# A spectral mixer and token MLP: Fourier transform along the sequence first, two global barriers, and an inverse that is streamed block by block into the first MLP tiles

## The chip, the cores and the metric

One core of one Trainium2 chip. The metric is the device time of one execution in microseconds (us), taken as the median of several executions on the same chip. The profile's span is about 2 us shorter than that time. A median below is over all four runs of a kernel. The record marks some of them as slow (over 1.5% above the fastest of the same kernel). A "look" is a single run, whose state is unknown. The experiments ran on three chips, on which the kernel before took 169.06 to 169.16 us.

Names used: PE is the matrix engine (TensorE), DVE the vector engine, ACT the scalar engine, POOL GpSimd, SP the engine used here to issue DMAs. SBUF is the on-chip working memory, PSUM the one that matmuls write to, and an eviction is the pass that brings a result from PSUM to SBUF. In chains, a name with q (ACTq) is the engine's instruction queue, here issuing a DMA and not computing, and "issue" is time for which the profile shows no wait. A barrier is a point at which a stage needs every block of the stage before.

## The reference

The input `x` has S = 2048 rows (sequence) and D = 512 columns. In short:

```python
h  = x + irfft2(rfft2(layernorm(x)) * (w_r + 1j * w_i))      # 2-D transform over S and D
n  = layernorm(layernorm(h))                                 # over D
u  = gelu(einsum("sd,sf->df", n, w1) + b1)                   # F = 1376, contracts over S
h2 = h + transpose(u @ w2 + b2)                              # back to S
```

In the kernels a row is s = 16·p + s2: partition p (128 of them) holds 16 rows, and most work goes by "s2 block" of 128 x 512 elements.

## The kernel before

It transforms along D first (matrix `E`, after transposing X on TensorE), then along S in two steps (`FP`, `G2`) with a second set of transposes between them, multiplies by the weights in SBUF, and goes back by `Hm`, `IFP` and `GD`. The residual is added by an extra matmul with the identity. A small list scheduler in the file fixes each engine's instruction order at build time. So at run time each engine works its list in order: in e6_early (below) DVE stood 7.56 us before a small conversion, and once that was moved back in the list (e8_bias_last) the addition behind it started at 60.4 us instead of 64.1. The parts that matter here:

```python
# statistics of X on DVE, 16 of them; apply is folded into the eviction of the first transform
K.op(f"ln{which}_stats{s2}", "dve", ... eng.bn_stats(st[:, s2, 0:6], src) ...)
...
# spectral multiply: six SBUF-to-SBUF passes for each quarter
K.op(f"wm{q}_t1", "dve", ... eng.tensor_tensor(o, a, b, ALU.mult) ...)   # Cr * Wr
... # t2, t3, t4
K.op(f"wm{q}_r", "dve", ... eng.tensor_tensor(o, a, b, ALU.subtract) ...)
K.op(f"wm{q}_i", "dve", ... eng.tensor_tensor(o, a, b, ALU.add) ...)
...
# weights: natural layout, 128 partitions, pieces of 257 elements (514 bytes)
dma("ld_wr", Wn[:, 0, :, :], A_w_r.rearrange("(k2 k1) k -> k1 k2 k", k1=NP), 1 << 20, stream="sp", ...)
dma("ld_wi", Wn[:, 1, :, :], A_w_i.rearrange("(k2 k1) k -> k1 k2 k", k1=NP), 1 << 20, stream="sp", ...)
...
# second norm: statistics for all 16 blocks, then apply on DVE or ACT, then MLP 1 tile by tile
K.op(f"ln23_apply{s2}", ("dve", "act"), emit_app, ...)
for t in range(NFT):            # 11 tiles of F
    for s2 in range(NS2):       # 16 matmuls of 512 columns, one PSUM bank
        K.op(f"mm1_{t}_mm{s2}", "pe", ...)
    ... # GELU on ACT and DVE
for s2 in range(NS2): ...       # MLP 2: 11 matmuls, one DVE pass, one store
```

Of the kernel before, what the change touches and what calls it, by code (L numbers as in the profile page):

```python
# [8 lines left out]

S_LEN = 2048
D_LEN = 512
NP = 128
NS2 = 16
NKC = 32
F_LEN = 1376
NFT = 11
GELU_C = 0.7978845608028654
LN_EPS = 1e-5


def _bf16(a):
    return np.asarray(a, dtype=np.float32).astype(dt.np(dt.bfloat16))


def build_consts():
    c = {}
    two_pi = 2.0 * np.pi
    d = np.arange(D_LEN)[:, None]
    k = (np.arange(256)[None, :] + 1)  # L30
    ang = two_pi * ((k * d) % D_LEN) / D_LEN
    E = np.concatenate([np.cos(ang), -np.sin(ang)], axis=1)
    c["E"] = E.reshape(4, NP, 512).transpose(1, 0, 2)
    n1 = np.arange(NP)[:, None, None]
    n2 = np.arange(NS2)[None, :, None]
    k1 = np.arange(NP)[None, None, :]
    s = 16 * n1 + n2
    ang = two_pi * ((k1 * s) % S_LEN) / S_LEN
    FP = np.zeros((NP, NS2, 3, NP), np.float64)
    FP[:, :, 0, :] = np.cos(ang)  # L40
    FP[:, :, 1, :] = -np.sin(ang)
    FP[:, :, 2, :] = np.sin(ang)
    c["FP"] = FP
    c["ID"] = np.eye(NP)
    G = np.zeros((NP, 3, NP), np.float64)
    for n2_ in range(NS2):
        for k2_ in range(NS2):
            a = two_pi * ((n2_ * k2_) % NS2) / NS2
            for kk in range(8):
                G[n2_ * 8 + kk, 0, k2_ * 8 + kk] = np.cos(a)  # L50
                G[n2_ * 8 + kk, 1, k2_ * 8 + kk] = -np.sin(a)
                G[n2_ * 8 + kk, 2, k2_ * 8 + kk] = np.sin(a)
    c["G2"] = G
    Hm = np.zeros((NP, 2, 256), np.float64)
    for k2_ in range(NS2):
        for s2_ in range(NS2):
            a = two_pi * ((k2_ * s2_) % NS2) / NS2
            hre, him = np.cos(a), np.sin(a)
            for kk in range(8):
                p = k2_ * 8 + kk  # L60
                col = s2_ * 8 + kk
                Hm[p, 0, col] = hre
                Hm[p, 0, 128 + col] = him
                Hm[p, 1, col] = -him
                Hm[p, 1, 128 + col] = hre
    c["Hm"] = Hm
    k1 = np.arange(NP)[:, None, None]
    s2 = np.arange(NS2)[None, :, None]
    s1 = np.arange(NP)[None, None, :]
    ang = two_pi * ((k1 * (16 * s1 + s2)) % S_LEN) / S_LEN  # L70
    ifr = np.cos(ang) / S_LEN
    ifi = np.sin(ang) / S_LEN
    IFP = np.zeros((NP, NS2, 2, 256), np.float64)
    IFP[:, :, 0, 0:128] = ifr
    IFP[:, :, 0, 128:256] = ifi
    IFP[:, :, 1, 0:128] = -ifi
    IFP[:, :, 1, 128:256] = ifr
    c["IFP"] = IFP
    kk = (np.arange(256)[:, None] + 1)
    dd = np.arange(D_LEN)[None, :]  # L80
    ang = two_pi * ((kk * dd) % D_LEN) / D_LEN
    fac = np.full((256, 1), 2.0 / D_LEN)
    fac[255, 0] = 1.0 / D_LEN
    Gc = fac * np.cos(ang)
    Gs = -fac * np.sin(ang)
    Gs[255, :] = 0.0
    GD = np.zeros((NP, 2, 2, D_LEN), np.float64)
    for half in range(2):
        GD[:, half, 0, :] = Gc[half * 128:(half + 1) * 128, :]
        GD[:, half, 1, :] = Gs[half * 128:(half + 1) * 128, :]  # L90
    c["GD"] = GD
    return c


_ENG_TYPE = {
    "pe": mybir.EngineType.PE,
    "act": mybir.EngineType.Activation,
    "dve": mybir.EngineType.DVE,
    "pool": mybir.EngineType.Pool,
    "sp": mybir.EngineType.SP,  # L100
}
_STREAMS = ["sp", "pe", "act", "dve", "pool"]
N_DMA_SEMS = 36
SB_CELL = 32
# [4 lines left out]
PSUM_BANKS = 8  # L109
PSUM_BANK_BYTES = 2048  # L110


class PsumUnit:

    def __init__(self, name, nbanks=1, early_ok=False):
        self.name = name
        self.nbanks = nbanks
        self.early_ok = early_ok
        self.bank = None
        self.ops = []  # L120
        self.claimed = False
        self.done = False


class Op:
    __slots__ = ("idx", "name", "engines", "stream", "lane", "reads", "writes", "dur", "emit",
                 "psum_unit", "psum_banks", "psum_is_first", "psum_is_last", "deps", "consumers",
                 "sched", "start", "finish", "eng", "increments", "lane_idx", "waits", "prio",
                 "bytes", "is_dma", "_psum_read", "_psum_write", "same_engine_as", "not_before")

    def __init__(self):
        self.deps = []
        self.consumers = []
        self.sched = False
        self.increments = False
        self.lane_idx = None
        self.waits = []
        self.psum_unit = None
        self.psum_banks = []
        self.psum_is_first = False  # L140
        self.psum_is_last = False
        self.prio = 0
        self.bytes = 0
        self.is_dma = False
        self._psum_read = False
        self._psum_write = False
        self.same_engine_as = None
        self.not_before = 0.0


class KernelBuilder:
    def __init__(self, nc):
        self.nc = nc
        self.ops = []
        self.cells = {}
        self.psum_cells = {}
        self.tensors = {}
        self.tensors_by_hname = {}
        self.inst_names = {}
        self.arena_base = None  # L160

    def setup_memory(self, layout, es):
        nc = self.nc
        base = ((nc.sbuf_base + 511) // 512) * 512
        total = nc.sbuf_top - base
        total = (total // 512) * 512
        self.arena_base = base
        self.arena_size = total
        self._slab = es.enter_context(nc.sbuf_tensor("arena_slab", [NP, total - 64], dt.uint8))
        for name, shape, dty, off in layout:  # L170
            size = int(np.prod(shape[1:])) * dt.size(dty)
            assert off % 32 == 0, (name, off)
            assert off + size <= total - 64, f"{name} overflows arena: {off}+{size} > {total}"
            h = nc.alloc_sbuf_tensor_at(name, list(shape), dty, offset=base + off)
            self.tensors[name] = (h, off, off + size)
            self.tensors_by_hname[h.name] = (h, off, off + size)
        return {n: self.tensors[n][0] for n in self.tensors}

    def sb_cells(self, ap):
        t = ap.tensor  # L180
        name = t.name
        if name not in self.tensors_by_hname:
            raise KeyError(name)
        h, lo, hi = self.tensors_by_hname[name]
        esz = dt.size(ap.dtype)
        offs = np.array([int(ap.offset)], dtype=np.int64)
        dims = list(ap.ap)[1:]
        for step, n in dims:
# [3 lines left out]
        byte_offs = lo + offs * esz  # L192
        cells_lo = byte_offs // SB_CELL
        cells_hi = (byte_offs + esz - 1) // SB_CELL
        if np.all(cells_lo == cells_hi):
            cells = np.unique(cells_lo)
        else:
            cells = np.unique(np.concatenate([cells_lo, cells_hi]))
        return cells

    def op(self, name, engines, emit, ins=(), outs=(), dur=100.0, lane=None, psum=None,
           psum_read=False, psum_write=False, psum_first=False, psum_last=False, prio=0,
           extra_deps=(), nbytes=0, is_dma=False, same_engine_as=None, not_before=0.0):
# [4 lines left out]
        o.stream = None  # L208
        o.lane = lane
# [5 lines left out]
        o.same_engine_as = same_engine_as  # L215
        o.not_before = not_before
        o.reads = []
        o.writes = []
        deps = set()
        for d in extra_deps:  # L220
            deps.add(d)
        for ap in ins:
            cells = self.sb_cells(ap)
            o.reads.append(cells)
            for c_ in cells:
                ci = int(c_)
                rec = self.cells.get(ci)
                if rec is not None:
                    if rec[0] is not None:
                        deps.add(rec[0])  # L230
                    rec[1].append(o)
                else:
                    self.cells[ci] = [None, [o]]
        for ap in outs:
            cells = self.sb_cells(ap)
            o.writes.append(cells)
            for c_ in cells:
                ci = int(c_)
                rec = self.cells.get(ci)
                if rec is not None:  # L240
                    if rec[0] is not None:
                        deps.add(rec[0])
                    for r in rec[1]:
                        if r is not o:
# [879 lines left out]
```

## Time and profile before

169.17 us (169.11 to 169.24). By stage, from the chain of waits:

| stage | ends at, us | held by |
|---|---|---|
| statistics of X | 19.2 | DVE |
| forward transforms | 45.1 | PE, evictions |
| spectral multiply | 59.6 | DVE |
| inverse transforms | 79.6 | PE |
| second norm | 90.4 | DVE |
| MLP 1 | 125.2 | PE |
| MLP 2 | 163.7 | PE |
| span | 167.1 | last eviction and store |

The page's first lines and its table of 40 slices. Each digit is a busy share in tenths, PEclk the TensorE clock that was granted, and the last row what the DMA engines moved:

```profile
span 167.1 us, 2513 instructions
PE 150.8 (90%) x912; PEld 90.8 (54%) x912; DVE 103.6 (62%) x251; ACT 75.8 (45%) x130; POOL 10.9 (6%) x23
...
PE   0599899998998689999995999999999999999991
PEclk9999999999999999999999999999999999999999
GB/s 98 372 355 299 404 46 127 45 322 141 4 2 229 277 184 411 389 367 219 4 99 399 129 2 0 0 4 0 0 0 0 63 67 63 33 61 63 63 33 61
```

PE has work everywhere, at the full clock (1.000 on average). Some pieces of the chain that ended last, in order of time (start, duration, what):

```profile
1.13 4.98 DMA X<-in_A_x_dram
...
19.20 0.67 DVE D_56 L747
...
59.01 0.61 DVE V_64 L846
...
90.42 34.72 PE ps L1009 x160
125.17 0.69 ACT U_105 L1014
...
128.35 35.26 PE ps L1033 x162
```

A 512-column matmul on this chain costs 34.72/160 = 0.217 us. The "mean ns" of the matmul groups (379 ns for the same shape) is the length of one while others overlap it, not its price: on the page 66 of them, 25.0 us laid end to end, keep PE busy for 16.6 us.

### The profile page before, as it was taken

What the parts mean: (1) busy time and instruction counts of PE and PEld (TensorE: products, weight loads), DVE (VectorE), ACT (ScalarE), POOL (GpSimd) and SP (SyncE); (2) the same over time, 40 slices, a digit from 0 to 9 for tenths busy, and PEclk for the clock granted to TensorE, in tenths of its full rate; (3) what the DMA queues carried; (4) which work ended last, traced back from release to release, by engine and by line L of the source; (5) the groups of instructions that cost most, each with busy time, mean ns of one, the idle gap of its engine ahead of it and who ended that gap; (6) DMA issues with size and microseconds to landing.
All of it is one profiled execution on the core that took longest, in us unless ns stands there. A gap on an engine that the chain in (4) does not pass through costs nothing.

```text
span 167.1 us, 2513 instructions
## 1 busy us (share of the span) xinstructions
PE 150.8 (90%) x912; PEld 90.8 (54%) x912; DVE 103.6 (62%) x251; ACT 75.8 (45%) x130; POOL 10.9 (6%) x23
## 2 busy tenths in 40 slices
PE   0599899998998689999995999999999999999991
PEld 0593346987546568544431444444455666666660
DVE  0599981987999979779998454354445322332231
ACT  3075897662599668456885644433432000000000
POOL 0000022200001070200060000000000000000000
PEclk9999999999999999999999999999999999999999
DMA  4999914283006659996039300000000111011101
GB/s 98 372 355 299 404 46 127 45 322 141 4 2 229 277 184 411 389 367 219 4 99 399 129 2 0 0 4 0 0 0 0 63 67 63 33 61 63 63 33 61
DMA packets 10123, 22.71 MB, mean 136 GB/s; under 512 B 928, under 2 KB 7328, under 8 KB 9472
## 3 DMA queue, kind: packets, MB, share of 16 engines
q0 software_dynamic: 2384, 13.90, 22.5%
q1 hardware_dynamic: 7728, 8.66, 15.9%
q8 instruction: 7, 0.11, 0.3%
q14 instruction: 4, 0.03, 0.1%
HBM read 20.46 MB, written 2.10 MB: 135 GB/s over the span
## 4 chain that ended last, share of the span: by engine, by line
PE 67%; DVE 24%; DMA 3%; ACT 3%; issue 1%; SPq 0%; ACTq 0%; DVEq 0%
PE ps L1033 21%; PE ps L1009 21%; DVE st_87 L657 6%; PE ps L918 6%; PE ps L738 5%; PE ps L769 4%; PE ps L892 4%; DMA X<-in_A_x_dram 3%; PE ps L797 2%; DVE st_89 L952 2%; PE ps L719 2%; DVE V_64 L846 1%; DVE V_64 L845 1%; PE ps L910 1%; PE ps L864 1%
## 5 line engine op out<-in xcount | busy, mean ns | idle before, releaser
L1038 DVE SCALAR_TENSOR_TENSOR OUT<-ps,B2f,H 128x512 bf16<-128x512 f32 x16 | 12.0, 751 | 24.2 <-PE ps L1033 24.2
L1009 PE MATMUL ps<-HH,W_b 128*128 128x512 bf16 (+1 forms) x66 | 16.6, 379 | 1.7 <-DVE HH L984 1.5
L918 PE MATMUL ps<-GD,V_51 128*128 128x512 bf16 x64 | 16.4, 379 | 0.0
L1009 PE MATMUL ps<-HH,W_a 128*128 128x512 bf16 (+1 forms) x66 | 16.1, 379 | 0.0
L738 PE MATMUL ps<-Esb,XT 128*128 128x512 bf16 x64 | 14.6, 380 | 1.0 <-DVE D_56 L747 0.6
L657 DVE BATCH_NORM_STATS2 st_87<-X 128x6 f32<-128x512 bf16 x16 | 9.9, 680 | 6.1 <-DMA X<-in_A_x_dram 6.1
L1009 PEld LDWEIGHTS ps<-HH,W_b 128*128 128x128 bf16 (+1 forms) x66 | 6.4, 100 | 10.0 <-DVE HH L984 2.2
L696 PE MATMUL ps<-ID,X 128*128 128x128 bf16 x64 | 6.1, 287 | 6.2 <-DMA X<-in_A_x_dram 6.2
L952 DVE BATCH_NORM_STATS2 st_89<-H 128x6 f32<-128x512 bf16 x16 | 10.8, 686 | 1.3 <-ACT H L926 1.0
L1009 PE MATMUL ps<-HH,W_c 128*128 128x512 bf16 (+1 forms) x44 | 11.3, 379 | 0.0
L738 PEld LDWEIGHTS ps<-Esb,XT 128*128 128x128 bf16 x64 | 5.8, 98 | 9.4 <-ACT XT L703 2.1
L1009 PEld LDWEIGHTS ps<-HH,W_a 128*128 128x128 bf16 (+1 forms) x66 | 6.5, 100 | 7.7 <-ACT HH L983 0.4
L926 ACT ACTIVATE H<-ps 128x512 bf16<-128x512 f32 x13 | 7.7, 595 | 6.4 <-PE ps L918 6.4
L864 PE MATMUL ps<-Hm,V_64 128*128 128x256 bf16 x64 | 8.2, 273 | 2.8 <-ACT TT L877 1.2
L918 PEld LDWEIGHTS ps<-GD,V_51 128*128 128x128 bf16 x64 | 6.2, 98 | 7.5
L830 ACT ACTIVATE Csb<-ps 128x512 bf16<-128x512 f32 x16 | 7.9, 680 | 4.3 <-PE ps L823 4.3
L877 ACT ACTIVATE TT<-ps 128x512 bf16<-128x512 f32 x16 | 8.5, 655 | 2.9 <-PE ps L864 2.8
L696 PEld LDWEIGHTS ps<-ID,X 128*128 128x128 bf16 x64 | 6.0, 134 | 6.2 <-issue 6.2
L864 PEld LDWEIGHTS ps<-Hm,V_64 128*128 128x128 bf16 x64 | 6.0, 98 | 5.0 <-ACT TT L877 2.1
L746 ACT ACTIVATE D_56<-ps,lnw_88 128x512 bf16<-128x512 f32 x13 | 8.1, 694 | 0.6 <-PE ps L738 0.4
L900 DVE CAST V_51<-ps 128x256 bf16<-128x256 f32 x19 | 7.2, 420 | 1.3 <-PE ps L892 1.2
L703 ACT ACTIVATE XT<-ps 128x1024 bf16<-128x1024 bf16 x8 | 7.6, 1017 | 0.0
(118 smaller groups left out, 274.5 us busy)
## 6 DMA issues: line engine op xcount, KB each, us to landing
W_a<-in_B_w_dram POOLq DMA_DIRECT2D x1, 2064.0 KB, 7.6
W_b<-in_B_w_dram POOLq DMA_DIRECT2D x1, 2064.0 KB, 10.4
X<-in_A_x_dram SPq DMA_DIRECT2D x4, 512.0 KB, 6.2
IFP<-c_IFP POOLq DMA_DIRECT2D x1, 2048.0 KB, 9.1
out_dram<-OUT SPq DMA_DIRECT2D x16, 128.0 KB, 1.7
FP<-c_FP SPq DMA_DIRECT2D x1, 1536.0 KB, 10.9
W_c<-in_B_w_dram POOLq DMA_DIRECT2D x1, 1376.0 KB, 6.1
Wn<-in_A_w_r_dram SPq DMA_DIRECT2D x1, 1028.0 KB, 11.0
```

What stands on the lines that cost most here:

```text
L657: o = K.op(f"ln{which}_stats{s2}", "dve", (lambda s, eng, bank, src=src, s2=s2: eng.bn_stats(st[:, s2, 0:6], src)), ins=[src], outs=[st[:, ...
L696: (lambda s, eng, bank, lhsT=lhsT, i=i: eng.matmul(psb[:, bank, i * 128:(i + 1) * 128], lhsT, ID[:, :], is_transpose=True, start=True, sto ...
L738: (lambda s, eng, bank, lhsT=lhsT, rhs=rhs, t=t: eng.matmul(ps[:, bank, :], lhsT, rhs, start=(t == 0), stop=(t == 3))),
L746: return eng.activation(dst, src, ACT.Copy, scale=sc)
L830: return eng.activation(dst, src, ACT.Copy)
L864: eng.matmul(ps[:, bank + ci // 2, (ci % 2) * 256:(ci % 2) * 256 + 256], lhsT, rhs, start=(comp == 0), stop=(comp == 1))),
L877: return eng.activation(dst, src, ACT.Copy)
L918: (lambda s, eng, bank, lhsT=lhsT, rhs=rhs, mi=mi: eng.matmul(ps[:, bank, :], lhsT, rhs, start=False, stop=(mi == 3))),
L952: K.op(f"ln2_stats{s2}", "dve", (lambda s, eng, bank, src=src, s2=s2: eng.bn_stats(st2[:, s2, 0:6], src)), ins=[src], outs=[st2[:, s2, 0:6 ...
L1009: (lambda s, eng, bank, lhsT=lhsT, rhs=rhs, s2=s2, Mt=Mt: eng.matmul(ps[0:Mt, bank, :], lhsT, rhs, start=(s2 == 0), stop=(s2 == NS2 - 1))),
L1033: (lambda s, eng, bank, lhsT=lhsT, rhs=rhs, t=t: eng.matmul(ps[:, bank, :], lhsT, rhs, start=(t == 0), stop=(t == NFT - 1))),
L1038: (lambda s, eng, bank, dst=dst, bia=bia, hs=hs: eng.scalar_tensor_tensor(dst, ps[:, bank, :], bia, hs, op0=ALU.add, op1=ALU.add)),
```

## The change

Its intent is to give PE less to do and to overlap the stages. The transform along S comes first, on real columns: each of 32 groups packs four real basis functions, so that no transpose is needed. The weights are multiplied straight out of PSUM. Because of the real basis the weights are needed twice, in natural order on partitions 0 to 63 and mirrored (row 64-g) on 64 to 127. A first barrier stands before the transform along D (it needs every block), a second one before the inverse. After the second, each s2 block streams through inverse, residual, norm and the first five MLP-1 tiles, which accumulate in five open PSUM banks. The diff is nearly a rewrite. Its core, with cuts marked:

```diff
-    # normalisation folded into the eviction of transform 1 (rstd only)
+def apply(which, src, dst, i, engines, prio):
+    K.op(f"ln{which}_ap{i}", engines, lambda ...: eng.tensor_scalar(dst, src, a, b, op0=ALU.subtract, op1=ALU.mult), ...)
 ...
+        apply(1, X[:, i, :], HN[:, i, :], i, ("pool",), 20)
 ...
-    dma("ld_wr", Wn[:, 0, :, :], A_w_r.rearrange("(k2 k1) k -> k1 k2 k", k1=NP), ...)
+    for g0, g1 in ((0, 8), (8, 32)):
+        n = (g1 - g0) * 257
+        for w, dram in ((0, A_w_r), (1, A_w_i)):
+            d = Wx[w][0:64, g0:g1, :]
+            dma(f"ld_w{w}p_{g0}", d, bass.AP(dram.tensor, g0 * 257, [[0, 2], [64 * 257, 32], [1, n]]), ...)
 ...
+            for comp in range(2):
+                d = Wx[w][64 + comp * 32:96 + comp * 32, h0:g1, :]
+                dma(f"ld_w{w}m{comp}_{g0}", d, bass.AP(dram.tensor, (64 - h0) * 257, [[64 * 257, 32], [-257, g1 - h0], [1, 257]]),
+                    ..., "act", ..., after=[X2])
 ...
-    # six tensor_tensor passes per quarter in SBUF
+    # two passes per eighth, PSUM x weights -> SBUF
+            return eng.tensor_tensor(ov, src, wv, ALU.mult)
 ...
+    for s2 in range(NS2):
+        ... # inverse along D, eviction on ACT, inverse along S
+        K.op(f"h_{s2}", "dve", ... eng.tensor_tensor(hs, ps[:, bank, :], xs, ALU.add) ...)
+        stats(2, H[:, s2, :], s2, 9)
+        rstd(2, slice(s2, s2 + 1), EPS[:, 1:2], 1.0 + LN_EPS, 10)
+        apply(2, H[:, s2, :], HH[:, s2, :], s2, ("pool",), 9)
+        for t in range(5):
+            mm1(t, s2)
```

## The prediction

> **What bounds it now.** The page gives PE 150.8 of 167.1 us at full granted clock. The chain of waits is PE for 67% and DVE for 24%. In order of time: DVE statistics of X until 19.2 us, PE transforms, a DVE stretch of spectral multiplies (45 to 59.6 us), PE transforms to 79.6, the second norm on DVE to 90.4, then PE without a gap: MLP 1 about 86.6 to 124.8, MLP 2 to 163.6, tail 3.5. On the chain a 512-column matmul costs 0.217 us (160 in 34.72), a 256-column one 0.109 (64 in 7.00), a 128-column transpose 0.058.
>
> **What the change does to the work.** Gone are 192 transposes, the separate residual matmuls and 21 us of multiply-passes from SBUF. PE before the MLPs falls from about 164,000 columns (70 us at the chain's rate) to 98,000 (42 us). Total PE floor falls from 146 to 118 us. MLP 2 (38.2 us) and the tail are unchanged. So the question is when the second barrier opens (T2), and how long MLP 1 takes from there.
>
> **First barrier.** X lands as before (about 6 us). DVE: 16 x (0.60 + about 0.19) with waits on ACT square roots that stand behind Y evictions and four DMA issues in ACT's queue. Normalising moves to POOL. [...] Sum: POOL ends about 26, Y evictions (1.02 us each) about 29 us.
>
> **Middle stage.** 16 CS evictions at about 0.62 us on ACT: 39 us. The instruction order then matters: ACT issues the large mirrored weight loads (1.58 MB in 514-byte pieces) only behind all 16 evictions. The old weight load of the same pieces moved 1.05 MB in 3.6 us, so they land about 44 (real) and 46 us (imaginary). DVE also waits for biases queued behind W1 (10.7 MB at the 420 GB/s of contiguous loads: about 31 to 35 us). Multiplies 2 to 7 can start only then: about 1.26 us each (slope of the evictions 256->420 ns, 512->690 ns), 12 of them: DVE ends about 59, T2 about 61. Without that late load T2 would be near 50: I expect about 10 us to be lost to it.
>
> **Inverse and MLP 1.** Per block DVE needs 0.70 + 0.68 + 0.17 + 0.1 = 1.65 us; ordering against POOL's previous apply (small statistics share cells) makes it about 1.9. PE has 2.0 us per block if MLP-1 work fills in, but its order gives only about 47 MLP matmuls before the last inverse block at about T2 + 30; 129 x 0.217 = 28 us follow. MLP 1 ends about 120 us, against 124.8 before.
>
> Span: 120 + 38.5 + 3.5 = 162; plus 2 us as before between span and time: **163 us** (0.964 of before), eight times in ten 153 to 172. Faster by over 2%: 0.67; within 2%: 0.22; slower: 0.11.
>
> **What would show it.** PE busy about 120-125 us, under 80% of span; a PE and DVE hole between about 33 and 45 us ended by the DMA of Wr/Wi; the x multiplies at 1.2 to 1.3 us; [...] aggregate instructions waiting on POOL; W1 landed before T2; a solid PE from about 92 us to the end; MLP-2 durations unchanged.
>
> **What would make it wrong.** If the mirrored weights come early, 150 to 153. [...] If the descending 514-byte loads are much slower than the old ones, 170 or more. PE stalls in the strict interleaving of the inverse stream could add some us.

The forecast came to 163 us: MLP 1 ends at 120, and MLP 2 (38.5) and the tail (3.5) make a span of 162, and with about 2 more this was put down as 163.

## The result

229.69 us (228.93 to 230.92, 4 runs) against 169.17: slower. The ratio is 1.3585 (95% interval 1.3537 to 1.3634). A ratio is the mean time of one kernel's fast runs over the mean of the other's of the same rounds, so it is not quite the ratio of the medians quoted.

The page after, the same lines as before:

```profile
span 229.1 us, 2043 instructions
PE 142.7 (62%) x784; PEld 78.9 (34%) x784; DVE 84.1 (37%) x179; ACT 60.7 (26%) x105; POOL 66.6 (29%) x38
...
PE   0044505459950000496797488664799999999994
PEclk9999999999996555599599979999599999999998
GB/s 210 391 71 324 252 366 266 52 31 55 56 137 63 54 139 32 60 299 319 285 31 0 0 0 0 3 0 0 0 0 0 4 0 46 46 59 59 46 69 46
```

PE's instructions did fall, from 912 to 784, but PE is now busy for 62% of a longer span. There are two long thin stretches: a head of 52 us in which PE works about a third of the time, and a hole from 65 to 94 us (29 us, of which PE worked 1.9). In the GB/s row there is a long plateau near 55, where the kernel before has no such stretch until its stores at the end. The chain that ended last:

```profile
5.88 24.99 DMA Wi<-in_A_w_i_dram
...
30.89 0.32 ACTq L515
...
31.76 0.31 ACT sd_95 L571
...
41.00 8.26 POOL HN L586 x4
...
49.95 1.95 ACT Y L526 x2
...
65.29 15.38 ACTq L515
80.67 0.04 issue
80.71 13.31 DMA Wi<-in_A_w_i_dram
...
108.03 1.24 DVE V L652
...
159.06 2.08 POOL HH L586
...
164.18 23.14 PE ps L520 x101
...
190.52 35.26 PE ps L520 x162
```

Two things fill it. The first is loads of the weights: 25 us at the head (two loads in ACT's list wait for this one to land, and the third group's square root stands behind them: ACT sat idle for 10.7 us before it), then 15.4 us in which ACT's queue cannot issue one (ACTq, no compute), then 13.3 us until it lands. The second is POOL: eight microseconds for four instructions in the head, and one instruction per block from 118 to 161 us. MLP 2 is as before, 35.26 us for 162 matmuls.

The groups of POOL, and the two-operation form on DVE that the kernel before used for the same job (line, engine, operation, shapes, count, busy us, mean ns, idle before and its cause). First after, then before:

```profile
L586 POOL TENSOR_SCALAR HH<-H,mv_98,rs_100 128x512 bf16<-128x512 bf16 x16 | 33.2, 2076 | 81.7 <-DVE rs_100 L573 81.7
L586 POOL TENSOR_SCALAR HN<-X,mv_94,rs_96 128x512 bf16<-128x512 bf16 x16 | 33.0, 2076 | 15.3 <-DVE mv_94 L580 14.9 <-DVE rs_96 L573 0.4
```

```profile
L984 DVE TENSOR_SCALAR HH<-H,lnw_92 128x512 bf16<-128x512 bf16 x7 | 2.4, 408 | 0.1
```

2.08 us on POOL against 0.41 us on DVE.

The DMA view of the kernel after between 52 and 64 us, in 40 slices of 0.3 us:

```profile
DMA  1211010010210100100100100100101001001001
GB/s 41 83 41 41 41 82 41 41 82 41 96 82 0 82 41 41 82 41 41 82 41 41 82 41 41 82 41 41 82 0 82 41 41 82 41 41 82 41 41 82
```

The engines are busy for about an eighth of their time (the view gives 13.1% for the main queue in this window), and move 55 GB/s on average. 13.1% of the view's 16 engines is the work of 2.1 engines. That two were busy and 14 idle is an estimate of mine from that figure: the view does not list the engines one by one. What these loads cost, e1_load16 tests.

### The profile page after: what moved, and what is told of

It is laid out like the page before. It is cut to its first block, busy times and chain, and to the rows that moved or that the text cites. A ratio compares the mean times of both kernels' runs of the same rounds, so it can differ in the third digit from the quotient of the medians.

```text
span 229.1 us, 2043 instructions
## 1 busy us (share of the span) xinstructions
PE 142.7 (62%) x784; PEld 78.9 (34%) x784; DVE 84.1 (37%) x179; ACT 60.7 (26%) x105; POOL 66.6 (29%) x38
## 4 chain that ended last, share of the span: by engine, by line
PE 33%; POOL 21%; DMA 17%; DVE 11%; ACTq 7%; ACT 5%; SPq 2%; issue 2%; POOLq 1%; DVEq 0%
PE ps L520 33%; DMA Wi<-in_A_w_i_dram 17%; POOL HH L586 14%; POOL HN L586 7%; ACTq L515 7%; DVE V L652 5%; ACT CS L526 3%; DVE H L702 3%; SPq L515 2%; DVE st_97 L578 1%; DVE mv_98 L580 1%; POOLq L749 1%; ACT Y L526 1%; DVE rs_100 L573 1%; DVE OUT L742 0%
## 5 line engine op out<-in xcount | busy, mean ns | idle before, releaser
L586 POOL TENSOR_SCALAR HH<-H,mv_98,rs_100 128x512 bf16<-128x512 bf16 x16 | 33.2, 2076 | 81.7 <-DVE rs_100 L573 81.7
L520 PE MATMUL ps<-HH,W_78 128*128 128x512 bf16 (+1 forms) x176 | 44.1, 401 | 8.6 <-POOL HH L586 5.6
L520 PE MATMUL ps<-FP,HN 128*128 128x256 bf16 x64 | 16.5, 413 | 33.8 <-POOL HN L586 33.8
L586 POOL TENSOR_SCALAR HN<-X,mv_94,rs_96 128x512 bf16<-128x512 bf16 x16 | 33.0, 2076 | 15.3 <-DVE mv_94 L580 14.9
L520 PE MATMUL ps<-EM,V 128*128 128x128 bf16 x128 | 12.1, 251 | 31.4 <-DVE V L652 30.5
L520 PEld LDWEIGHTS ps<-HH,W_78 128*128 128x128 bf16 (+1 forms) x176 | 17.8, 104 | 30.5 <-POOL HH L586 6.6
L520 PE MATMUL ps<-EO,IF 128*128 128x256 bf16 (+1 forms) x48 | 10.7, 335 | 5.6 <-DVE H L702 4.1
L702 DVE TENSOR_TENSOR H<-ps,X 128x512 bf16<-128x512 f32 x16 | 10.6, 664 | 5.6 <-PE ps L520 5.6
L520 PE MATMUL ps<-EM,PQ 128*128 128x256 bf16 x64 | 10.3, 300 | 2.0 <-ACT EO L526 1.3
L520 PE MATMUL ps<-EM,Y 128*128 128x256 bf16 x64 | 10.6, 314 | 1.0 <-ACT Y L526 1.0
L580 DVE BATCH_NORM_AGGREGATE mv_98<-st_97 128x2 f32<-128x6 f32 x16 | 2.9, 182 | 20.2 <-POOL HH L586 20.1
## 6 DMA issues: line engine op xcount, KB each, us to landing
W_78<-in_B_w_dram SPq DMA_DIRECT2D x4, 1376.0 KB, 25.5
IF<-c_IF SPq DMA_DIRECT2D x1, 1024.0 KB, 19.1
```

What stands on the lines that cost most here:

```text
L520: return eng.matmul(outf(bank), lhsT, rhs, start=start, stop=stop, **({"skip_group_check": True} if skip else {}))
L580: K.op(f"ln{which}_ag{i}", "dve", lambda s, eng, bank: eng.bn_aggr(mv[:, i, :], st[:, i, 0:6]), ins=[st[:, i, 0:6]], outs=[mv[:, i, :]], d ...
L586: K.op(f"ln{which}_ap{i}", engines, lambda s, eng, bank: eng.tensor_scalar(dst, src, a, b, op0=ALU.subtract, op1=ALU.mult), ins=[src, a, b ...
L702: K.op(f"h_{s2}", "dve", lambda s, eng, bank, xs=xs, hs=hs: eng.tensor_tensor(hs, ps[:, bank, :], xs, ALU.add), ins=[xs], outs=[hs], dur=6 ...
```

## The experiments

Theory: two costs that the prediction had mis-sized make up the loss. (A) The weight loads whose source pattern begins with a dimension of size 2 move only 55 GB/s, on two DMA engines by the estimate above. (B) The normalising instruction on POOL costs 2.08 us. Rivals: the mirrored loads are slow because they descend or are in 514-byte pieces; only one of the two matters and the other hides behind it; something else (the PE clock, or stalls in the strict order) is missing as well. Unless said otherwise, results are correct.

### e1_load16: only the loads

```diff
-            dma(..., d, bass.AP(dram.tensor, g0 * 257, [[0, 2], [64 * 257, 32], [1, n]]), ...)      # d: partitions 0..63
+            for c in range(2):                                                                     # d: 32c..32c+31
+                dma(..., d, bass.AP(dram.tensor, g0 * 257, [[64 * 257, 32], [1, n]]), ...)
```

The single-row loads for partitions 64 to 127 are cut the same way.

> Edit: only the four kinds of weight loads whose source pattern starts with a dimension of size 2 are cut into two loads of 32 partitions each; everything else of the changed kernel stays. Theory A (these loads run on two DMA engines only: the trace shows a plateau of 53 GB/s at a DMA busy share of 0.1): the plateau is gone, the late weights land before 66 us instead of 94, DVE multiplies end near 79 us instead of 109, the second barrier moves from about 112 to about 81 us, time 195 to 202 us. Rival B (the descending 514-byte pieces are slow by themselves): they still take 13 to 20 us from issue to landing, time 205 to 216 us. Rival C (POOL paces all, loads hide behind it): time over 222 us.

Measured: 207.6 us (206.77 to 210.31), ratio to before 1.2335 [1.2252, 1.2418]. The 210.31 is slow; the ratio lies above all three fast runs (206.77 to 207.63) and so must contain it. Fast runs alone give 1.226. The page's DMA rows:

```profile
DMA  6999999910069669980000000000000001211111
GB/s 187 413 273 430 406 384 167 200 24 3 0 103 138 69 210 311 272 304 11 0 0 0 0 0 3 0 0 0 0 0 5 0 26 54 74 53 53 51 51 53
```

The plateau is gone: until the stores at the end nearly every DMA stretch is over 60% busy or idle, and ACT no longer blocks when it issues (1.7 us for the last two loads instead of 17.8). The first barrier came at 46.4 us instead of 51.9, the second at 88.7 instead of 111.6 (I had written about 81). So A is confirmed as a cost of 22 us; the number of engines is not shown by this run either. But the time lies in the range that was written for rival B, not for A, although the landing time written for B, 13 to 20 us, was not met either. The late mirrored loads landed at 70.7 us (I had written before 66), 11.9 us after the wait for them began on the chain. They were still slow for a reason that this run does not tell. Rival C falls.

### e2_dve_apply: only the normalising instruction

```diff
-            apply(1, X[:, i, :], HN[:, i, :], i, ("pool",), 20)
+            apply(1, X[:, i, :], HN[:, i, :], i, ("dve",), 20)
-        apply(2, H[:, s2, :], HH[:, s2, :], s2, ("pool",), 9)
+        apply(2, H[:, s2, :], HH[:, s2, :], s2, ("dve",), 9)
```

> Edit: only the 32 normalising instructions move from POOL (2.08 us each in the trace) to DVE (0.41 us for the same form in the kernel before); loads stay as in the change. If POOL and the loads are two separate costs: the first barrier moves from 52 to about 43 us, but weights still land at about 87 to 94 us [...], the second barrier opens at 104 to 111 us, the inverse stage takes about 35 us instead of 52, time 203 to 212 us. If POOL alone is the cause (loads late only because they are issued late): time 165 to 180 us. If loads alone are: over 222 us.

Measured: 210.81 us (209.98 to 211.95), ratio 1.2476 [1.2431, 1.2521], inside the range for two separate costs. The first barrier moved to 44.2 us. The weights still land at 93.1 us; a piece of its chain:

```profile
69.61 23.45 DMA Wi<-in_A_w_i_dram
93.13 1.24 DVE V L652
```

In the inverse stream a block now takes 1.91 us in place of about 3.1.

### e3_both: both

> Both edits. Theory: the two costs are all that the prediction missed, so the stage sums of the prediction come back: first barrier about 29 us, late weights land about 45, second barrier about 61, about 2.0 us per block in the inverse stage, time 158 to 170 us, centre 163. If something else was missed as well (PE clock, interleaving stalls, slow descending loads) the time stays over 175 us.

Measured: 172.66 us (172.21 to 174.3), ratio 1.0232 [1.018, 1.0284], still behind the kernel before (the interval crosses 2%, so the class is unclear). Loads alone gave 22 us, POOL alone 19, both together 57. The second barrier shows where the other 16 us lie: it came at 111.6 us in the kernel after, 88.7 in e1_load16, 110.9 in e2_dve_apply and 72.5 here. POOL's cost in the head is hidden behind the late loads and comes to light only when these are mended. The time is 3 us outside the range written for "nothing else was missed", and 2 us short of the one for "something was". The chain shows that something was:

```profile
42.84 11.88 DMA Wi<-in_A_w_i_dram
54.72 0.04 DVEq L421
54.75 0.04 issue
54.80 1.24 DVE V L654
56.03 0.05 issue
56.08 5.05 PE ps L520 x41
61.12 1.23 DVE V L654
```

The late weights land at 54.7 us, where the prediction had 46. Then DVE waits once more for 5 us, because PE's fixed order has the inverse matmuls of the first groups ahead of the next multiply's own. The multiplies end at 70.8 us instead of 59.

### e4_pool_forms: what POOL charges (wrong result on purpose, one look)

```diff
+            if which == 1 and i < 8:  return eng.tensor_scalar(dst, src, b, None, op0=ALU.mult)
+            if which == 1:            return eng.tensor_copy(dst, src)
+            if i < 8:                 return eng.tensor_scalar(dst, src, 0.5, 1.5, op0=ALU.subtract, op1=ALU.mult)
+            return eng.tensor_tensor(dst, src, src, ALU.add)
```

> Measures POOL by itself, wrong results on purpose: the 128x512 bf16 normalising instruction is replaced on POOL by four forms, eight of each: one operation with a per-partition scalar; a plain copy; two operations with immediates; tensor plus tensor. If 2.08 us is the cost of two operations: the one-operation form takes about 1.0 to 1.2 us and the immediates form stays at 2.0 to 2.1. If it is the cost of fetching per-partition scalars: immediates take under 1 us. If it is a floor of any POOL pass over 512 bf16 elements (type conversion, loop): copy takes about 2 us too. [...]

POOL's instructions in order of time (start, us, instruction, count, idle before):

```profile
10.07 6.19 POOL L588 TENSOR_SCALAR HN<-X,rs 128x512 bf16<-128x512 bf16 x4 [9.10 <-DVE mv L580]
...
31.64 2.27 POOL L590 COPY HN<-X 128x512 bf16<-128x512 bf16 x4 [8.83 <-DVE mv L580]
...
120.04 1.92 POOL L592 TENSOR_SCALAR HH<-H 128x512 bf16<-128x512 bf16 x1 [0.94 <-DVE rs L573]
...
140.98 1.04 POOL L593 TENSOR_TENSOR HH<-H 128x512 bf16<-128x512 bf16 x1 [1.01 <-DVE rs L573]
```

Per instruction of 128x512 elements: copy 2.27/4 = 0.57 us, tensor plus tensor 1.04, one operation with a per-partition scalar 6.19/4 = 1.55, two operations with immediates 1.92, two with per-partition scalars 2.08 (in the kernel after). None of my three expectations fits. (The tensor form read the same tile as both inputs.) The second operation adds only about 0.5 us, and per-partition scalars in place of immediates 0.16. The scalar form itself is dear on POOL, even with one operation. Why the form is dear these runs do not show.

### e5_ascend and e7_contig: why the mirrored loads stay slow (wrong results on purpose, one look each)

```diff
-    [[64 * 257, 32], [-257, g1 - h0], [1, 257]]      # e3_both: descending rows, 514-byte pieces
+    [[64 * 257, 32], [2 * 257, g1 - h0], [1, 257]]   # e5_ascend: ascending, 514-byte pieces
+    [[64 * 257, 32], [1, (g1 - h0) * 257]]           # e7_contig: one run of 12336 bytes
```

> Both repairs as in e3_both, and the mirrored weight loads read every second row in ascending order (wrong result on purpose; same 514-byte pieces, same 32 partitions, same issue places). In e3_both the four large mirrored loads took about 12 us from the last issue (42.8) to landing (54.7), 1.58 MB, where the kernel before moved 514-byte pieces to 128 partitions at 290 GB/s. If the descending order is what makes them slow: the last one lands about 6 us after its issue, at 48 to 50 us, and the time falls by 4 to 6 us. If not: landing stays at 53 to 56 us and the time within 1.5 us of e3_both (172.7).

> As e5_ascend, but each partition's piece is one contiguous run of 12336 bytes (wrong result on purpose; same bytes, same 32 partitions). If the small pieces are what is slow: the last load lands within 5 to 6 us of its issue (48 to 49 us). If it is the 32-partition destination or the competition with the other weight loads: landing stays at 53 to 56 us.

Measured: 174.22 us for e5_ascend, with the last weights landing at 56.0 us: the direction does not matter. 171.5 us for e7_contig, landing at 51.6 us, 10 us after the wait began (41.6 us; 42.8 in e3_both), between the two ranges that I had written: the size of the pieces accounts for about 2 of 12 us. Neither is the main cause.

### e10_wide: the same bytes over 128 partitions (wrong result on purpose, one look)

It builds on e8_bias_last below, and is told here because it answers the same question.

```diff
-    ... ten loads per weight matrix, 32 partitions each
+    d = Wx[w][:, g0:g1, :]
+    dma(..., d, bass.AP(dram.tensor, g0 * 257, [[8 * 257, 128], [1, n]]), ...)
```

> As e8_bias_last, but the same number of weight bytes (4.2 MB) is loaded by four loads over all 128 partitions with contiguous runs (wrong result on purpose). It measures the rate. In e6_early and e7_contig loads into 32 partitions ran at about 120 to 190 GB/s whether their runs were 514 or 12336 bytes. If the 32-partition destination is what holds them down: the slices behind X and the constants show 370 to 430 GB/s and the weights land by about 24 us. If it is the source rows: 160 to 190 GB/s stays. The time should change by less than 2 us unless late weights still hold up the multiplies.

They landed by about 22 us. The GB/s rows of the DMA view while weights were loading, in order: kernel before, 11 to 19 us (514-byte pieces, 128 partitions, until another load follows at three quarters of the row); e3_both, 43 to 54 us, with the engines' busy share (514-byte pieces, 32 partitions); e10_wide, 12 to 24 us (long runs, 128 partitions).

```profile
GB/s 332 337 324 314 306 303 293 290 293 290 288 293 296 290 296 288 298 293 290 293 290 288 293 293 290 290 290 293 600 341 239 566 289 507 430 369 492 369 553 246
```

```profile
DMA  9999999999999999999999999999999999952211
GB/s 137 133 136 135 131 142 136 133 140 136 140 138 135 135 133 148 136 148 133 142 136 142 131 131 140 138 135 133 140 129 140 133 131 103 116 52 28 34 24 28
```

```profile
GB/s 411 439 439 439 411 439 439 439 439 439 439 439 439 411 439 384 439 439 411 384 439 384 411 411 384 439 439 439 411 411 410 383 437 437 382 410 437 465 448 422
```

In e7_contig (long runs, 32 partitions) the mirrored loads moved 1.28 MB between 42 and 48 us, 213 GB/s; over 40 to 52 us the mean is 163, but that takes in the tail. Away from start and tail this makes a table:

| GB/s | 514-byte pieces | long runs |
|---|---|---|
| 128 partitions | 290 | 424 |
| 32 partitions | 135 | 213 |

Going from 32 to 128 partitions doubles the rate in both columns; longer runs give 1.5 to 1.6 times. In e3_both's stretch the engines were over 90% busy, so gaps between loads are not the reason. But the loads to 128 partitions were also fewer and larger (four of 1028 KB in e10_wide, against at most 386 KB each), and no run separates that from the partitions. e10_wide took 160.94 us in its one run, 2.6 us above the fast runs of e8_bias_last (158.1 and 158.6) and 0.4 above its slow ones: faster weights, landed by 22 us, bought nothing once they were asked for early.

### e6_early: ask for the mirrored weights early

```diff
-    for g0, g1 in ((0, 8), (8, 32)):
+    for g0, g1 in ((0, 16), (16, 32)):            # a boundary that no two loads share in the dependency grid
-        dma(f"ld_w{w}m{comp}_{g0}", ..., "act", outs=[d], prio=28, after=[X2])
+        dma(f"ld_w{w}m{comp}_{g0}", ..., outs=[d], prio=28)      # SP's queue, ahead of IF and W1
```

> Both repairs, correct result; the mirrored loads go on SP's queue with the other weights, ahead of the inverse matrix and W1, cut at row group 16 so that no two loads share a dependency cell; nothing else moves by hand. Theory (what is left of the loss in e3_both is the multiplies waiting for late mirrored weights, 44 to 61 us): all weights land by about 32 us, multiplies run without a DMA wait from about 35 to 55 us, second barrier about 56 us instead of 72.5, the rest 98 us as in e3_both: time 153 to 160 us, centre 156, faster than the kernel before. Rival (the multiplies' stage is paced by PE at half clock and by evictions, not by weights): second barrier after 62 us, time over 163 us.

Measured: 161.24 us (161.1 to 161.38), ratio 0.9531 [0.9515, 0.9547]: faster than the kernel before. The multiplies ran from 34.8 to 56.2 us without waiting for weights, as expected, and the second barrier opened at 57.9. The low clock of the rival was not there: it was 1.00 from 32 to 56 us (0.76 in e3_both from 44 to 72.5 us). The time is 1 us above the range, and DVE's timeline shows a wait that I had not foreseen here (the prediction had one for biases behind W1):

```profile
54.96 1.22 DVE L655 TENSOR_TENSOR V<-ps,Wi 128x1024 bf16<-128x1024 f32 x1
56.10 0.17 DVE L717 CAST B2f<-B2s 128x16 f32<-128x16 bf16 x1
63.83 0.17 DVE L714 CAST B1f<-B1s 128x10 f32<-128x10 bf16 x1 [7.56 <-DMA B1s<-in_B_b_dram]
```

A conversion of ten bias columns, which nothing needs before the GELU, stands in DVE's order ahead of the whole inverse stream and waits for a 0.2 KB load behind the W2 loads.

### e8_bias_last: the conversions behind the second norm

```diff
+    xl = [o for o in K.ops if o.name == "ln2_rs15"]
-    K.op("b1f_a", "dve", ..., dur=80.0)
+    K.op("b1f_a", "dve", ..., dur=80.0, after=xl)                # likewise b1f_b and b2f
```

> As e6_early, and the three small bias conversions on DVE are placed behind the second norm instead of ahead of it (they are first read by the GELU). In e6_early DVE sat 7.6 us at 56.3 to 63.8 us before a bias load of 0.2 KB that is queued behind the W2 loads. If that wait was on the path: the first residual addition starts at about 60 us (when its matmuls are done) instead of 64.1, time falls by 3.5 to 4.5 us to 156.5 to 158. If PE had slack to hide it: time stays at 160.5 to 161.5.

Measured: 159.53 us (158.07 to 160.56), ratio 0.9454 [0.9393, 0.9514]. In the profiled run the first residual addition started at 60.4 us instead of 64.1, as expected, and the span fell by 3.2 us. The median fell by only 1.7, but two of the four runs (160.5 and 160.56) are slow. The fast ones, 158.07 and 158.56, are 2.9 us under e6_early, still a little less than the 3.5 to 4.5 that I had written. The ratio lies above both fast runs and so must contain slow ones; fast runs alone give 0.936. Where the slow ones lose stays open: their clock, 0.978, is above that of the fast ones (0.956 and 0.962).

### e9_root_first: the square root ahead of the evictions

```diff
+    evac(f"f1_{q}_{b}_ev", "act", ..., after=[x for x in K.ops if x.name == f"ln1_sd{4 * q + 4}"])
```

> As e8_bias_last, and each group's square root is placed ahead of the previous group's Y evictions in ACT's order. In e6_early DVE waits 1.4 to 1.6 us in three of the four groups for a square root that stands behind two 1-us evictions. If this is on the path to the first barrier: the last Y eviction ends near 28 us instead of 32, time 3 to 4.5 us under e8_bias_last, about 153. If the weights (all landed by about 36 us) now hold the multiplies back, the gain is under 2 us.

Measured: 154.63 us (153.15 to 156.72), ratio 0.9114 [0.9069, 0.916]. The last Y eviction ends at 27.7 us (32.5 in e8_bias_last). Fast runs against fast runs, the median is 154.54 against 158.3 us: 3.8 us less, within what was expected. (All runs together would give 4.9; one of these four and two of those are slow.) This is the fastest version, 8.9% under the kernel before, with the algorithm of the change unaltered:

```profile
span 152.9 us, 2035 instructions
PE 127.5 (83%) x775; PEld 77.2 (50%) x784; DVE 95.6 (63%) x211; ACT 60.6 (40%) x105; POOL 0.4 (0%) x6
...
PE   0027885899996599999998699999999999999990
PEclk9999999999999959999999999999999999999999
```

## Why the prediction was wrong, point by point

| event (us from the start) | predicted | after | e3_both | e9_root_first |
|---|---|---|---|---|
| first barrier (last Y eviction ends) | 29 | 51.9 | 32.8 | 27.7 |
| last weights land | 46 | 94.0 | 54.7 | not awaited |
| last multiply ends | 59 | 109.3 | 70.8 | 51.8 |
| second barrier | 61 | 111.6 | 72.5 | 53.6 |
| MLP 1 ends (last tile's first GELU step) | 120 | 187.3 | 128.1 | 110.6 |
| span | 162 | 229.1 | 170.4 | 152.9 |

- **What held.** PE's work fell as counted (775 to 784 instructions in the runs, 127 us busy in e9_root_first against 118 for the floor), the multiplies cost 1.22 us against 1.26, MLP 2 and the tail are unchanged. That ACT issues the large mirrored loads only behind its evictions, and that DVE then waits for them, was predicted and seen. The predicted wait for biases was there too: in the kernel after, a bias conversion held DVE until 87.1 us, just ahead of the weights' own landing. So was POOL's grip on the statistics: 20.1 us of aggregate instructions waiting for POOL.
- **The first failed step: the price of POOL's normalising instruction.** POOL took 2.08 us for each, 33.0 us for the 16 of the head and 33.2 us for the 16 of the inverse stream. The sum had POOL done with the head at about 26 us; it ended at 49.3. With the loads mended, taking the form off POOL gave 35 us (207.6 to 172.66). The lower price that I used came from no trace or run. e4_pool_forms shows what a timing would have told: 1.55 us or more for every scalar form, against 0.57 for a copy.
- **The second failed step: "they land about 44 (real) and 46 us (imaginary)".** This had two mis-sized terms. The loads with a leading dimension of 2 were taken at 420 GB/s, the rate of the kernel before's contiguous loads (424 GB/s there between 16.4 and 20.2 us). I hadn't looked at their access pattern. The trace shows 13.1% of the DMA capacity busy and 55 GB/s, and without the leading 2 (e1_load16, which also cuts each of these loads in two) the time fell by 22 us. Why such loads are slow no run shows. And other loads stood behind them: W1 took 25.5 us to land against 18.3 in e3_both, the inverse matrix 19.1 against 9.8, a bias load of 0.2 KB 36.1 against 8.5, and one issue instruction held ACT for 16.1 us (at most 1.9 in e3_both). Long holds are not peculiar to these loads, though: in e3_both one issue held SP's queue for 19.1 us. The mirrored loads themselves were taken at the 290 GB/s of the old ones. But the old ones went to 128 partitions and these go to 32. The runs show 135 (514-byte pieces) and 213 GB/s (long runs) for loads to 32 partitions against 290 and 424 to 128, though with smaller loads on the 32.
- **A smaller one: full clock.** The head's sum used 0.109 us per 256-column matmul. In the last of the four groups of the head, 14 of them took 3.04 us in e3_both, where the granted clock was 0.79 on average over the first 33 us, against 1.72 in e9_root_first, whose PEclk row shows 9 throughout the head. No run here isolates what lowers the clock. e9_root_first's first three groups took 3.5 to 3.6 us for 16 too, although the profile shows full clock there, so the shown clock is not the whole account. The slow matmuls are part of the 3.8 us by which e3_both misses the predicted first barrier. The square roots behind the evictions, which the prediction named without pricing, are probably the rest. e9_root_first changes both, so I can't split them.
- **Where 57 of the 67 us went.** e3_both undoes POOL and the loads with a leading 2, leaving the mirrored loads at 32 partitions and late. That leaves 9.7 us over the prediction, where the last multiply is 11.8 us late (8.7 of it late weights: asked for 3.8 us later than predicted, and 4.9 us longer under way), partly made good by a faster MLP 1 (56 us from the second barrier in place of 59).

The kernel before lost none of this, because its first normalisation rode on an eviction, its second ran on DVE and ACT, and its weights came in two loads over 128 partitions. What the change gains shows once the other engines are fed: in e9_root_first PE is busy for 23.3 us less than before, and the time is 14.5 us less.

## What to carry to other kernels

Before you trust a load, write down the leading dimension of its source pattern and the number of partitions that it fills: here loads with a leading 2 cost 22 us, and loads to 32 partitions, smaller ones too, ran at about half the rate of loads to 128 (135 against 290 GB/s, 213 against 424). A DMA busy share that stands at a small fixed fraction (here 13.1%) while someone waits is the sign. A price for an instruction that no trace has timed on that engine is not an estimate but a bet, so time it alone first. And in a kernel with fixed orders look at what stands ahead of each wait: a bias conversion, a load issue or a square root in the wrong place cost 3 to 11 us here each.
